# Pairing the probability-times-value matmuls of two sets, and adding zero-weight matmuls, in a planned attention kernel

## Chip, cores, metric

One core of one Trainium2 chip. The time is device microseconds of one execution; each experiment was executed several times on a chip, beside the kernel before. A program on one core gets its state (fast or slow) from its own spread; all executions quoted here are fast ones, except one of e2's four, which was slow and is left out, and the single execution of e3, whose state is unknown. The granted clock is the share of full TensorE speed in the profile's records, 1.00 or 0.50. In the profile PE is TensorE, PEld its weight loads, ACT ScalarE, DVE VectorE and POOL GpSimd.

## The reference, cut to what matters

```python
# B=1, S=2048, D=512, H=32 heads of Dh=16; inputs and weights normal * 0.05, bf16
q, k, v = split(x @ A_wqkv)
a = softmax(q k^T * Dh**-0.5) v  @ A_wo           # full attention, 32 heads x 2048 x 2048
b = attention over 8 keys at distance 0,2,..,14 @ B_wo   # local, dilated
g = sigmoid((x * gate_w).sum(-1, keepdims=True))
out = g * a + (1 - g) * b
```

Full attention is 32 x 2048 x 2048 exponentials. The work is cut in 32 periods (a chunk of 512 queries times a group of four heads). A period has 64 units, each 128 keys x 512 queries of one head.

## The kernel before

A small event-driven planner in Python (class `Plan`) runs while the program is built. Jobs are generators; they ask for an engine with a priority and a planned duration, and the order in which the planner serves them becomes the fixed program order of each engine. The timelines below show PE in that order, and semaphores in the built program keep the data right.

- Scores (QK). Sets of three and of two units alternate. The matmuls of one set stand in different 32-row strips of the array and run together: in the trace of the kernel before the three of a set start within 9 ns (median), and at half clock three take 0.61 us by the profile, a single one 0.60. Three PSUM banks hold a three-unit set ("ring" A), two hold a two-unit set (ring B); each ring exists once, so the next scores of three wait until the exponential of the last three has ended.
- Exponential on ScalarE (ACT), 1536 or 1024 columns at once, into a tile `pT`.
- PV. The matmuls of a set stand in different 32-column strips (three start within 7 ns, median), and accumulate in one bank `acc`. Below, QK3 and PV2 are the scores of a three-unit set and the PV of a two-unit set, and so on.
- Projections (the matmuls that make q, k and v from x, and the output) are put in between where the plan finds room.
- A fourth unit ("rider") may go to VectorE (DVE), which computes its exponential in four operations into a tile `pd`.

```python
class Plan:
    def advance(self, gen, t, val):       # resume a job whose own time is t
        while True:
            req = gen.send(val)
            ...
            if op == "wait":              # an event: later of the two times
                ...; t = max(t, ev.time); continue
            if op == "now":
                val = t; continue
            ...                           # an engine: stand in its list, ready at t
            self.ready[eng].append([prio, self.seq, t, gen, dur, fn, ...]); return

    def run(self):
        while True:
            ...                           # choose engine and job with the earliest start st
            self.now = st
            ...
                x[5]()                    # fn: emits the instructions
                self.free[nm] = st + x[4]
                self.advance(x[3], st + x[4] + self.LAT[nm], None)   # at once, with a time to come

    def pv_job(p, items, res, prio, act=True):
        yield ("wait", ev_acc[p])
        for t, j, _ in items:
            yield ("wait", ev_v[(i, t)])
        dur = SW + MM                     # 0.11 for a change of kind + 0.22 for a stream
        def f():
            ...                           # the set's matmuls, and finished pd units of other strips
        yield ("pe", prio, dur, f)
        yield ("rel", res[0], res[1])     # give the pT tile back

    def act_tail(k, parts, rname, rslot, ring, n):
        ...
        yield ("act", k, 0.074 + 0.4267 * n, f)           # the exponential
        yield ("rel", rname, rslot)
        for q_, (p, us) in enumerate(parts):
            yield ("spawn", pv_job(p, items, ...))
```

Of the kernel before, what the change touches and what calls it, by code (L numbers as in the profile page):

```python
# [47 lines left out]
class Plan:  # L48
# [11 lines left out]
        self.now = 0.0  # L60

    held = {"job": 0}
    cap_job = 2
    refill = 0.56
    patience = 6.0
# [18 lines left out]
    def advance(self, gen, t, val):  # L84
        while True:
# [40 lines left out]
            self.ready[eng].append([prio, self.seq, t, gen, dur, fn, req[4] if len(req) > 4 else None, t])  # L126
            return

    def gate(self, need):

        if need is None:
            return 0.0
        if not self.slots[need] or self.held["job"] >= self.cap_job:
            return None
        return min(x[0] for x in self.slots[need])
# [8 lines left out]
    def run(self):  # L144
        while True:
            best = None
            for e, lst in self.ready.items():
                rs = []
                for x in lst:
                    g_ = self.gate(x[6])  # L150
                    if g_ is not None:
                        rs.append(max(x[2], g_))
                if rs:
                    st = max(self.free[e], min(rs))
                    if best is None or st < best[0]:
                        best = (st, 1, e)
            for r, lst in self.reqs.items():
                if lst and self.slots[r]:
                    st = max(min(x[0] for x in self.slots[r]), min(x[2] for x in lst))
                    if best is None or st <= best[0]:  # L160
                        best = (st, 0, r)
            if best is None:
                return
            st, kind, nm = best
            self.now = st
            if kind == 0:
                lst = self.reqs[nm]
                x = min(y for y in lst if y[2] <= st + 1e-9)
                lst.remove(x)
                s = min(y for y in self.slots[nm] if y[0] <= st + 1e-9)  # L170
                self.slots[nm].remove(s)
                self.advance(x[3], st, s[1])
            else:
                lst = self.ready[nm]
                ok = [y for y in lst if y[2] <= st + 1e-9 and self.gate(y[6]) is not None
                      and self.gate(y[6]) <= st + 1e-9]
                x = min(ok, key=lambda y: (y[0], y[1]))
                if nm == "pe" and not self.fits(x, st):
                    for y in ok:
                        y[2] = max(y[2], st + 0.1)  # L180
                    continue
                lst.remove(x)
                if x[6] is not None:
                    slot = self.take(x[6], st)
                    self.held["job"] += 1
                    x[5](slot)
                else:
                    x[5]()
                if CFG_DEBUG:
                    LOG.append((st, x[4], nm, getattr(x[3], '__name__', '?'), x[0]))  # L190
                self.free[nm] = st + x[4]
                self.advance(x[3], st + x[4] + self.LAT[nm], None)
# [3 lines left out]
def kernel(  # L196
# [53 lines left out]
    def mm(out_, lhsT, rhs, start, stop, **kw):  # L250
        return PE.matmul(out_, lhsT=lhsT, rhs=rhs, start=start, stop=stop, **kw)
# [21 lines left out]
    z32 = const.tile([128, 32], BF16, name="z32")  # L273
    ones_t = const.tile([128, QW], BF16, name="ones_t")
# [47 lines left out]
    P = Plan(["pe", "act", "dve", "pool", "sp"])  # L322
# [10 lines left out]
    P.resource("accS", 2)  # L333
    MM = 0.22
    SW = 0.11
    VP = 0.66
    EXP_PRIO = 60

# [12 lines left out]
    NP = len(periods)  # L351
# [4 lines left out]
    ev_v = {}  # L356
# [15 lines left out]
    def k_job(i, sc, rel, prio):  # L372
# [5 lines left out]
        def pe(s):  # L378
            w.open(s, [128, QW])
            for c in range(DC):  # L380
                mm(w.t[:], wkp[:, c, i].rearrange("p j d -> p (j d)"), xT[:, c, sc * QW:(sc + 1) * QW],
                   c == 0, c == DC - 1)
        yield ("pe", prio, 4 * MM + SW, pe, "w")
        kt = kt_all[:, i, sc * QW:(sc + 1) * QW]
        yield ("dve", prio, VP, lambda: V.tensor_scalar(out=kt, in0=w.t[:], scalar1=kbias[:, 0:1], scalar2=None,
                                                        op0=ALU.add))
        yield w.close()
        yield ("dve", prio, VP, lambda: V.tensor_reduce(out=kmax_all[:, i, sc:sc + 1], in_=kt, axis=AX.X,
                                                        op=ALU.max, apply_absolute_value=True))
# [12 lines left out]
    def v_job(h0, h1, tb, TB, rel, prio):  # L402
# [18 lines left out]
        for t0 in range(0, TB, step):  # L421
            yield ("pe", prio, one * step + SW, pe(t0, t0 + step)) + (("w",) if t0 == 0 else ())
        yield ("dve", prio, VP, lambda: V.tensor_copy(out=vp_all[:, tb:tb + TB, h0:h1, 0:DH],
                                                      in_=w.t[:].rearrange("p t (h d) -> p t h d", d=DH)))
# [7 lines left out]
    def q_job(p, rel, prio):  # L432
# [8 lines left out]
        def pe(s):  # L441
            w.open(s, [128, QW])
            for c in range(DC):
                mm(w.t[:], wqp[:, c, i].rearrange("p j d -> p (j d)"), xT[:, c, c_ * QW:(c_ + 1) * QW],
                   c == 0, c == DC - 1)
        yield ("pe", prio, 4 * MM + SW, pe, "w")
        st = {}

        def absq():
            st["a"] = work.tile([128, QW], BF16, name="absq", tag="absq", bufs=1)  # L450
            hi = w.t[:].bitcast(I16).rearrange("p (n two) -> p n two", two=2)[:, :, 1]
            V.tensor_scalar(out=st["a"][:].bitcast(I16), in0=hi, scalar1=0x7FFF, scalar2=None, op0=ALU.bitwise_and)
        yield ("dve", prio, VP, absq)
        yield ("wait", ev_sel[i])
        yield ("pe", prio, MM + SW, lambda: mm(w.t[:], selk_all[:, i, :], st["a"][:], False, True,
                                               skip_group_check=True))

        def evac():
            qt = work.tile([128, QW], BF16, name="qt", tag="qt", bufs=3)
            V.tensor_scalar(out=qt[:], in0=w.t[:], scalar1=QSC, scalar2=qbias[:, 0:1], op0=ALU.mult, op1=ALU.add)  # L460
            qt_tiles[p] = qt
        yield ("dve", prio, VP, evac)
        yield w.close()
# [32 lines left out]
    act_left = [4 * NT] * NP  # L496
    row_left = [[NT] * 4 for _ in range(NP)]
    pdq = [[] for _ in range(NP)]
    nset = [0]
    ndve = [0]  # L500
    DV_MIN = 12
    flying = [0]

    def rem(p):
        return sum(len(d) for d in pend[p])

    def ready(ev, t):
        return ev.time is not None and ev.time <= t
# [5 lines left out]

    def pv_job(p, items, res, prio, act=True):

        i = periods[p][1]
        yield ("wait", ev_acc[p])
        for t, j, _ in items:
            yield ("wait", ev_v[(i, t)])  # L520
        dur = SW + MM

        def f():
            if p not in acc_tiles:
                acc_tiles[p] = ps.tile([128, QW], FP32, tag="acc", bufs=1, name="acc")
                for c4 in range(4):
                    mm(acc_tiles[p][32 * c4:32 * c4 + 32], z32[:], ones_t[:], True, False,
                       tile_position=(0, 32 * c4))
            acc = acc_tiles[p]
            now = P.now  # L530
            if act:
                act_left[p] -= len(items)
            js = [j for _, j, _ in items]
            todo = list(items)
            for e in list(pdq[p]):
                if e[0] <= now and (act_left[p] == 0 or e[2] not in js) and ready(ev_v[(i, e[1])], now):
                    pdq[p].remove(e)
                    js.append(e[2])
                    todo.append(e[1:4])
                    P.slots["pd"].append((now + dur, e[4]))  # L540
            if act_left[p] == 0:
                for e in pdq[p]:
                    P.spawn(pv_job(p, [e[1:4]], ("pd", e[4]), 0.9, False), e[0])
                pdq[p].clear()
            for t, j, pt in todo:
                pv_left[p] -= 1
                row_left[p][j] -= 1
                mm(acc[32 * j:32 * j + DH + 1, :], vp_all[:, t, 4 * i + j, :], pt, False, row_left[p][j] == 0,
                   tile_position=(0, 32 * j))
        yield ("pe", prio, dur, f)  # L550
        yield ("rel", res[0], res[1])
        if pv_left[p] == 0:
            pv_left[p] = -1
            yield ("spawn", post_job(p))
# [19 lines left out]
    def act_stream():  # L574
        while front[0] < NP:
# [28 lines left out]
            ring = ps.tile([128, 3 if k % 2 == 0 else 2, QW], FP32, tag=rname, bufs=1, name="ring")  # L604
            dur = SW + MM

# [38 lines left out]
    def dve_unit(p, t, j, s, ds, wt, n):  # L645
# [8 lines left out]
        def e23(a):  # L654
            ta = st["ta"]
            V.scalar_tensor_tensor(out=ta[:], in0=ta[:], scalar=a, in1=lo, op0=ALU.add, op1=ALU.mult)
        yield ("dve", pr, VP - 0.05, e1)
        yield ("dve", pr, VP - 0.05, lambda: e23(A2))
# [369 lines left out]
    if CFG_DEBUG:  # L1028
        import os
        import pickle  # L1030
        pickle.dump(LOG, open("/tmp/plan.pkl", "wb"))
        left = {k: [(y[0], y[3].__name__) for y in v] for k, v in P.ready.items() if v}
        left.update({k: [(y[0], y[3].__name__) for y in v] for k, v in P.reqs.items() if v})
        print("plan ends", {e: round(v, 1) for e, v in P.free.items()}, "dve units", ndve[0], "sets", nset[0], left)
        if os.environ.get("PLANONLY"):
            raise SystemExit

# [34 lines left out]
```

## Time and profile before

| | before |
|---|---|
| time, median of 2 | 999.62 us |
| mean granted clock | 0.827 |
| first exponential / tail after the last one | 36 us / 12 us |
| ACT's gaps in between, summed from starts and ends in the trace | 100.4 us |
| of these, gaps that ended while the clock was half | 45.6 us |
| pair of exponentials (3 + 2 units), median at full clock | 2.25 us (2.235 us without a projection) |

A gap is counted whole, by the clock at its end, and the stretch before the first clock record as half clock. By the share of each gap that lay in half clock it is 63.5 us.

The head of the profile page of the kernel before (a third execution, 1004.99 us): span, busy time per engine, and three rows of the picture in 40 slices (busy tenths of PE and ACT, granted clock in tenths).

```profile
span 1003.2 us, 14401 instructions
...
PE 856.1 (85%) x5408; PEld 271.8 (27%) x5408; DVE 745.7 (74%) x1282; ACT 856.1 (85%) x759; POOL 582.6 (58%) x543
...
PE   2888899988889789898888888999888888888995
...
ACT  0479489898989989988989998899898999998895
...
PEclk9998979899977878868687988667778888887686
```

PE and ACT are equally busy on paper, but a busy PE at half clock is a slow PE: scores and the PV behind them start 0.54 us apart there (490.54 and 491.08 us), 0.32 at full clock (457.94 and 458.26 us). ACT is what bounds: 371 pairs at 2.235 us are 829 us. The groups of instructions of the kernel before (busy us, mean ns | idle before, and who ended most of it):

```profile
L241 ACT ACTIVATE pT<-ring 128x1536 bf16<-128x1536 f32 x741 | 851.2, 1257 | 121.5 <-PE ring L241 54.5
L241 PE MATMUL ring<-qt,kt_all 32*128 32x512 bf16 x1853 | 339.3, 449 | 109.1 <-ACT pT L241 105.2
L241 PE MATMUL acc<-pT,vp_all 128*17 128x512 bf16 x1853 | 334.1, 446 | 1.1 <-ACT pT L241 1.1
```

The timeline of PE in the kernel before, at half clock (start us, duration us, instruction, count, and in brackets the idle time before it):

```profile
490.54 0.61 PE L241 MATMUL ring<-qt,kt_all 32*128 32x512 bf16 x3
491.08 0.60 PE L241 MATMUL acc<-pT,vp_all 128*17 128x512 bf16 x3
491.62 0.61 PE L241 MATMUL ring<-qt,kt_all 32*128 32x512 bf16 x2
492.16 0.60 PE L241 MATMUL acc<-pT,vp_all 128*17 128x512 bf16 x2
492.80 0.61 PE L241 MATMUL ring<-qt,kt_all 32*128 32x512 bf16 x3
```

Read the starts: QK3, PV3, QK2, PV2 come 0.54 us apart. The pair repeats after 2.26 us, of which 4 x 0.54 = 2.16 us are used, so at half clock a projection (four matmuls, 1.82 us from 461.06 us to the next scores) finds no room and holds ACT up (the exponential at 463.59 us came after a gap of 1.18 us).

And the clock changes in steps: in the clock records of this trace all changes lie whole multiples of 3.413 us apart. Stretches of 3.41 us of the kernel before, cut where the clock records change (PE busy, weight loads, DVE, ACT, POOL, then the granted clock):

```profile
457.16:460.57 3.41, 1.94 (x21) 0.79 (x19) 2.65 (x4) 3.41 (x4) 3.41 (x4) 1.00 0.00 0
460.57:463.99 3.41, 3.41 (x18) 0.72 (x15) 2.38 (x4) 2.23 (x3) 3.33 (x4) 0.50 0.00 0
463.99:467.40 3.41, 3.21 (x27) 1.03 (x25) 2.67 (x5) 3.32 (x4) 3.18 (x4) 1.00 0.05 20
```

Here a step in which PE was busy 1.94 of 3.41 us is followed by one at half clock, in which a projection comes and ACT is busy only 2.23 us; that step, with PE busy throughout, is followed by full clock again.

### The profile page before, as it was taken

The numbers are of one execution on the slowest core, as the hardware profiler recorded it, in microseconds if no ns is written. First come the engines' busy times: TensorE is split into PE (matmuls) and PEld (weight loads), VectorE is DVE, ScalarE is ACT, GpSimd is POOL, SyncE is SP. The second block draws the span as 40 slices with busy tenths as digits, with TensorE's granted clock in tenths as the row PEclk, the third lists the DMA queues.
The fourth block names the chain that finished last, engine by engine and source line by source line (L and its number), as shares of the span: only waits on it lengthen the run. The fifth ranks groups of instructions, "written<-read, shape, count | busy, mean of one in ns | idle before, by whom it ended". The sixth has DMA issues, their size and how long they took to land.

```text
span 1003.2 us, 14401 instructions
## 1 busy us (share of the span) xinstructions
PE 856.1 (85%) x5408; PEld 271.8 (27%) x5408; DVE 745.7 (74%) x1282; ACT 856.1 (85%) x759; POOL 582.6 (58%) x543
## 2 busy tenths in 40 slices
PE   2888899988889789898888888999888888888995
PEld 1332433222222222222222222222222222222221
DVE  3566877586778777778877877887777776788775
ACT  0479489898989989988989998899898999998895
POOL 4004694300976928689739598829394949493600
PEclk9998979899977878868687988667778888887686
DMA  9004010001220020313100330202003020310000
GB/s 252 1 2 147 1 43 2 1 12 42 95 80 26 12 90 11 95 48 90 49 11 1 100 95 6 96 1 65 31 1 95 6 74 32 100 43 1 1 1 22
DMA packets 50006, 47.09 MB, mean 47 GB/s; under 512 B 9984, under 2 KB 47360, under 8 KB 49936
## 3 DMA queue, kind: packets, MB, share of 16 engines
q1 hardware_dynamic: 46240, 41.98, 13.8%
q10 hardware_dynamic: 3696, 4.20, 1.5%
q8 instruction: 42, 0.69, 0.3%
q14 instruction: 28, 0.23, 0.1%
HBM read 37.75 MB, written 6.32 MB: 44 GB/s over the span
## 4 chain that ended last, share of the span: by engine, by line
PE 41%; ACT 34%; issue 16%; DVE 6%; DMA 2%; SPq 0%; ACTq 0%; DVEq 0%
ACT pT L241 34%; PE ring L241 13%; PE acc L241 12%; DMA xT<-in_A_x_dram 2%; DVE ta L241 2%; DVE accS L241 1%; DVE kt_all L241 1%; ACT lg L241 0%; DVE vp_all L241 0%; DVE qt L241 0%; DVE lg L241 0%; DVE pd L241 0%; DVE kmax_all L241 0%; PE w_3662 L241 0%; PE w_9217 L241 0%
## 5 line engine op out<-in xcount | busy, mean ns | idle before, releaser
L241 ACT ACTIVATE pT<-ring 128x1536 bf16<-128x1536 f32 x741 | 851.2, 1257 | 121.5 <-PE ring L241 54.5
L241 PE MATMUL ring<-qt,kt_all 32*128 32x512 bf16 x1853 | 339.3, 449 | 109.1 <-ACT pT L241 105.2
L241 PE MATMUL acc<-pT,vp_all 128*17 128x512 bf16 x1853 | 334.1, 446 | 1.1 <-ACT pT L241 1.1
L241 POOL TENSOR_TENSOR prod<-vsh,lg 128x512 f32<-128x512 bf16 x128 | 136.6, 1099 | 195.6 <-issue 133.0
L241 POOL TENSOR_TENSOR prod<-prod 128x512 f32<-128x512 f32 (+1 forms) x208 | 240.0, 1167 | 6.3
L241 POOL TENSOR_TENSOR prod<-ksh,qb 128x512 f32<-128x512 bf16 x128 | 143.7, 1155 | 155.2 <-DVE qb L241 143.6
L241 PEld LDWEIGHTS <-kt_all 32*128 32x128 bf16 x2048 | 104.4, 93 | 349.0 <-issue 343.4
L241 PEld LDWEIGHTS <-vp_all 128*17 128x17 bf16 x2048 | 70.4, 89 | 205.1 <-issue 203.6
L241 PE MATMUL acc<-pd,vp_all 128*17 128x512 bf16 x195 | 86.7, 471 | 0.0
L241 PEld LDWEIGHTS <-xT 128*128 128x128 bf16 x512 | 36.0, 109 | 45.0 <-issue 36.4
L241 DVE COPY accS<-acc 128x512 f32<-128x512 f32 x32 | 22.0, 687 | 8.2 <-PE acc L241 7.6
L241 DVE TENSOR_REDUCE kmax_all<-kt_all 128x1 f32<-128x512 bf16 x32 | 21.7, 679 | 0.4
L241 PEld LDWEIGHTS <-wkp 128*128 128x128 bf16 x128 | 11.1, 104 | 37.1 <-issue 18.0
L241 POOL TENSOR_TENSOR obb<-ob,prod 128x512 bf16<-128x512 f32 x16 | 20.3, 1272 | 1.2
L241 POOL TENSOR_TENSOR ob<-prod 128x512 f32<-128x512 f32 x16 | 20.3, 1269 | 1.3
L241 PEld LDWEIGHTS <-wqp 128*128 128x128 bf16 x128 | 12.3, 115 | 26.1 <-issue 20.3
L241 PE MATMUL acc<-ones_t,z_85 128*32 128x512 bf16 x128 | 15.2, 464 | 1.0 <-DVE accS L241 0.5
L241 POOL TENSOR_TENSOR lg<-prod 128x128 f32<-128x128 f32 x32 | 13.7, 429 | 2.5
L241 ACT ACT_TABLE_LOAD x1 | 1.3, 1283 | 12.2 <-DMA xT<-in_A_x_dram 12.2
L241 PE MATMUL w_136<-xT,wkp 128*128 128x512 bf16 x4 | 1.9, 619 | 11.3 <-DMA xT<-in_A_x_dram 11.3
L241 DVE TENSOR_TENSOR lg<-lg,mx 128x256 f32<-128x256 f32 x16 | 9.0, 561 | 0.1
L241 DVE RECIPROCAL rden<-rden 128x16 f32<-128x16 f32 x32 | 8.0, 249 | 0.6
(1390 smaller groups left out, 1143.7 us busy)
## 6 DMA issues: line engine op xcount, KB each, us to landing
ksh<-kv_scr SPq DMA_DIRECT2D x16, 1024.0 KB, 5.8
vsh<-kv_scr SPq DMA_DIRECT2D x16, 1024.0 KB, 7.3
kv_scr<-kvs SPq DMA_DIRECT2D x16, 256.0 KB, 2.0
out_dram<-osb SPq DMA_DIRECT2D x16, 128.0 KB, 1.7
bw<-in_B_wqkv_dram ACTq DMA_DIRECT2D x1, 1536.0 KB, 14.5
wraw<-in_A_wqkv_dram ACTq DMA_DIRECT2D x2, 512.0 KB, 6.2
wv<-in_A_wqkv_dram ACTq DMA_DIRECT2D x1, 512.0 KB, 10.1
bwo<-in_B_wo_dram ACTq DMA_DIRECT2D x1, 512.0 KB, 8.1
```

The lines of the kernel that those rows point to most:

```text
L241: return chain_on(self._key, f(*a, **k))
```

## The change

Its intent: PV groups of three and two units become one group of five (two rounds in the column strips), so that PE changes less often between row-tiled and column-tiled matmuls; and where a group starts and PE has streamed little in the last 3 us of the plan, one matmul with zero weights is added, to keep the clock up.

```diff
+    streamed = deque()
+    def quiet(self, window):
+        while self.streamed and self.streamed[0][0] < self.now - window:
+            self.streamed.popleft()
+        return sum(d - 0.11 for _, d in self.streamed)
 ...
+    WARM = 0.47
+    held_pv = [[] for _ in range(NP)]
 ...
     def pv_job(p, items, res, prio, act=True):
         ...
+        if act:
+            act_left[p] -= len(items)
+            if len(items) == 3 and act_left[p] > 0:
+                held_pv[p].append((items, res))
+                return
         dur = SW + MM
+        fin = [res]
         def f():
 ...
+                for its, r in held_pv[p]:
+                    todo = list(its) + todo
+                    fin.append(r)
+                held_pv[p].clear()
 ...            (the group's matmuls, in rounds; finished pd units where a round has room)
+            extra = MM * (max(cnt) - 1)
+            if P.quiet(3.0) + MM * max(cnt) < WARM * 3.0 and max(row_left[p]) > 0:
+                j = max(range(4), key=lambda j_: row_left[p][j_])
+                mm(acc[32 * j:32 * j + 32, :], z32[:], ones_t[:], False, False, tile_position=(0, 32 * j))
+                extra += MM
+            return extra
         yield ("pe", prio, dur, f)
-        yield ("rel", res[0], res[1])
+        for r in fin:
+            yield ("rel", r[0], r[1])
```

In the program order, which can be read before any run, the runs of one matmul kind on PE fall from 1687 to 1214, zero matmuls rise from 128 (they open each accumulator) to 137, sets fall from 741 to 737 and VectorE units rise from 195 to 206.

More of the change, by code (lines that the diff above doesn't have):

```diff
@@ L185, in run @@
                     self.held["job"] += 1
-                    x[5](slot)
+                    more = x[5](slot)
                 else:
-                    x[5]()
+                    more = x[5]()
+                if isinstance(more, float):
+                    x[4] += more
+                if nm == "pe":
+                    self.streamed.append((st, x[4]))
                 if CFG_DEBUG:
@@ L502 @@
     flying = [0]
+    njunk = [0]
+    held_pv = [[] for _ in range(NP)]
     def rem(p):
@@ L530, in f @@
             now = P.now
+            todo = list(items)
             if act:
-                act_left[p] -= len(items)
-            js = [j for _, j, _ in items]
-            todo = list(items)
+                for its, r in held_pv[p]:
+                    todo = list(its) + todo
+                    fin.append(r)
+                held_pv[p].clear()
+            cnt = [sum(1 for x in todo if x[1] == j) for j in range(4)]
+            most = max(cnt)
             for e in list(pdq[p]):
-                if e[0] <= now and (act_left[p] == 0 or e[2] not in js) and ready(ev_v[(i, e[1])], now):
+                if e[0] <= now and (act_left[p] == 0 or cnt[e[2]] < most) and ready(ev_v[(i, e[1])], now):
                     pdq[p].remove(e)
-                    js.append(e[2])
+                    cnt[e[2]] += 1
                     todo.append(e[1:4])
-                    P.slots["pd"].append((now + dur, e[4]))
+                    fin.append(("pd", e[4]))
             if act_left[p] == 0:
@@ L544, in f @@
                 pdq[p].clear()
-            for t, j, pt in todo:
+            seen = [0] * 4
+            order = []
+            for x in todo:
+                order.append((seen[x[1]], x))
+                seen[x[1]] += 1
+            for _, (t, j, pt) in sorted(order, key=lambda y: y[0]):
                 pv_left[p] -= 1
@@ L549, in f @@
                    tile_position=(0, 32 * j))
+            extra = MM * (max(cnt) - 1)
[3 more added lines that the diff above has]
+                extra += MM
+                njunk[0] += 1
+            return extra
         yield ("pe", prio, dur, f)
-        yield ("rel", res[0], res[1])
+        for r in fin:
+            yield ("rel", r[0], r[1])
         if pv_left[p] == 0:
@@ L1033 @@
         left.update({k: [(y[0], y[3].__name__) for y in v] for k, v in P.reqs.items() if v})
-        print("plan ends", {e: round(v, 1) for e, v in P.free.items()}, "dve units", ndve[0], "sets", nset[0], left)
+        print("plan ends", {e: round(v, 1) for e, v in P.free.items()}, "junk", njunk[0], "dve units", ndve[0], "sets", nset[0], left)
         if os.environ.get("PLANONLY"):
```

## The prediction

> **What bounds the kernel now.** ScalarE's exponentials. In the engine table PE and ACT are each busy 856 of 1003 us; by start times in the trace a pair of exponentials (three units, then two) repeats every 2.235 us while the clock is full (1.331 + 0.904 us, medians), so 371 pairs need about 829 us. The stretches by window show no exponential before 36 us, and 12 us of tail. ACT's gaps between sum to 100 us: 26 before 150 us (12.4 of it in one stall at 101 us), 35 later at full clock, 40 later at half clock. PE is late: the waits view names PE's ring first.
>
> Mean granted clock 0.827, changing in steps of 3.41 us. Counting columns streamed per step (concurrent matmuls merged) against the full-rate maximum: half-clock steps up to 0.39 stay cold, those above about 0.41 are followed by full clock; full-clock steps below about 0.40 by half clock. [...] Four streams of 0.213 us per 2.26 us are 0.38, so a stretch without projection work falls cold, and the next projection (four matmuls, 1.82 us cold) then holds ACT up by 1.2 to 1.7 us.
>
> **What the change does.** (a) In program order QK3, PV3, QK2, PV2 becomes QK3, QK2, PV5. Streams stay the same (PV5 takes two rounds), but the runs of one matmul kind on PE fall from 1687 to 1214. In the timeline, streams of different kinds start 0.32 us apart warm and 0.54 cold, against 0.215 and 0.43 for the same kind, so a change costs about 0.11 us [...]. Estimate: 473 x 0.11 = 52 us less PE time. Only late stretches count: a backlogged cold pair falls from 2.16 to 1.94 us.
> (b) Zero matmuls: ones_t matmuls go from 128 to 137, so nine were added. As a PV group starts, the planned last 3 us already hold enough.
> (c) Sets fall from 741 to 737, DVE units rise from 195 to 206: about 5 us less ACT work.
> (d) Against: QK2 and two PV rounds now stand together. Cold, about 1.5 us from QK2's start to the next QK3, while ACT releases that ring after about 1.35 us: an estimated 0.08 us lost per cold pair that has no projection, some 6 us.
> (e) Streaming is lumpier (one stream, then three), so some cold steps should rewarm and some warm ones fall. Clock roughly 0.83 to 0.88.
>
> **Sum.** Of about 100 us ACT gaps roughly 30 should go, 5 us less ACT work, 6 us given back: about 970 us, 3% faster. Range 952 to 988. Chances: faster by over 2%: 0.72; within 2%: 0.26; slower: 0.02.
>
> **Signs.** ACT gaps total 65 to 80 us, losing most at half clock; first exponential still at 36 us; "PE ring" waits shrink; nine more zero matmuls; QK-to-QK starts 0.43 cold; clock not raised by more than 0.06; cold no-projection pairs at about 2.3 us instead of 2.26.
>
> **What would make it wrong.** If cold steps grow more frequent (clock under 0.80), projections meet half clock more often and the gain vanishes. If rewarming is much easier, the gain is larger (below 952). If held PV groups delay the accumulator's hand-over, or P tiles run out, ACT waits on PV.

"Cold" is half clock, "warm" full clock. The limits of 0.39 to 0.41 are my count in the trace of the kernel before, put too sharply: the steps overlap, half-clock ones rose from 0.36 on and stayed up to 0.44 (figures in the last section).

## More of the kernel before

The experiments ran on four different chips; the kernel before had medians of 1000.9 to 1002.9 us beside them.

Score matmuls wait for ACT (the ring must come free); PV matmuls wait for practically nothing, 1.1 us in the whole run: when PE comes to them, their probabilities are already there.

## The result

| | before | after |
|---|---|---|
| time, median of 2 | 999.62 us | 1151.2 us |
| mean granted clock | 0.827 | 0.765 |
| ACT's gaps | 100.4 us | 225.6 us |
| of these, ended at half clock | 45.6 us | 134.4 us |
| pair, median at full / half clock | 2.25 / 2.26 us | 2.54 / 3.18 us |

The ratio is 1.152 (95% interval 1.147 to 1.157). Ratios here are the mean time of one kernel's fast runs over that of the other's of the same rounds, so they are not quite the ratio of the medians. Executions over 1.5% slower than the fastest of the same kernel are left out of the means.

The same head of the page, changed kernel:

```profile
span 1148.8 us, 14309 instructions
...
PE 832.3 (72%) x5351; PEld 238.6 (21%) x5417; DVE 766.2 (67%) x1326; ACT 876.9 (76%) x755; POOL 582.5 (51%) x543
...
PE   3878776787788677677767776767678776667775
...
ACT  0577877887778878877778877778788877877794
...
PEclk8589988988768957766578967658688966766695
```

PE and ACT are now both idle a quarter of the time. Two engines that idle that much may be waiting for each other in turn, and the groups and the chain below show that here they are. The same three groups:

```profile
L252 ACT ACTIVATE pT<-ring 128x1536 bf16<-128x1536 f32 x737 | 872.0, 1236 | 247.8 <-PE ring L252 149.0
L252 PE MATMUL acc<-pT,vp_all 128*17 128x512 bf16 x1842 | 294.3, 471 | 252.5 <-ACT pT L252 251.9
L252 PE MATMUL ring<-qt,kt_all 32*128 32x512 bf16 x1842 | 329.2, 469 | 23.0 <-ACT pT L252 21.8
```

The wait has moved. Before, scores waited for ACT (105 us) and PV for nothing; now PV waits 252 us for an exponential and scores hardly wait, because they stand behind PV in PE's order. PE of the changed kernel in the timeline, at half clock:

```profile
506.45 0.60 PE L252 MATMUL acc<-pT,vp_all 128*17 128x512 bf16 x4 [1.18 <-ACT pT L252]
...
507.41 1.03 PE L252 MATMUL ring<-qt,kt_all 32*128 32x512 bf16 x5
509.57 1.03 PE L252 MATMUL acc<-pT,vp_all 128*17 128x512 bf16 x5 [1.13 <-ACT pT L252]
510.53 1.03 PE L252 MATMUL ring<-qt,kt_all 32*128 32x512 bf16 x5
```

And ACT of the changed kernel in the timeline, in the same stretch:

```profile
504.95 2.37 ACT L252 ACTIVATE pT<-ring 128x1536 bf16<-128x1536 f32 x2 [1.24 <-PE w_4972 L252]
508.07 2.37 ACT L252 ACTIVATE pT<-ring 128x1536 bf16<-128x1536 f32 x2 [0.76 <-PE ring L252]
```

The two exponentials of a pair merge into one line, the three-unit one first. The scores of both sets are done at 508.4 (507.41 + 1.03); then PE stands still until 509.57, just after the end of the *three-unit* exponential that began at 508.07 and took 1.46 us, and only then runs the PV group, and the next scores after it. The chain of waits of the changed kernel shows the cycle:

```profile
508.07 1.46 ACT pT L252
509.57 1.03 PE acc L252 x5
510.60 0.57 PE ring L252 x3
511.20 0.04 issue
511.25 1.46 ACT pT L252
```

508.07 to 511.25 is 3.18 us: three-unit exponential, PV group, scores, one after the other; only the two-unit exponential runs beside the PV group. A group of set k and set k+1 need not wait there: set k+2's exponential is the one that it waits for.

### The profile page after: what moved, and what is told of

It reads as the page before. It is cut to its first block, busy times and chain, and to the rows that moved or that the text cites. A ratio compares the mean times of both kernels' runs of the same rounds, so it can differ in the third digit from the quotient of the medians.

```text
span 1148.8 us, 14309 instructions
## 1 busy us (share of the span) xinstructions
PE 832.3 (72%) x5351; PEld 238.6 (21%) x5417; DVE 766.2 (67%) x1326; ACT 876.9 (76%) x755; POOL 582.5 (51%) x543
## 4 chain that ended last, share of the span: by engine, by line
PE 49%; ACT 41%; issue 5%; DVE 2%; DMA 2%; ACTq 0%; SPq 0%; DVEq 0%
ACT pT L252 41%; PE acc L252 22%; PE ring L252 14%; DMA xT<-in_A_x_dram 2%; DVE ta L252 1%; DVE accS L252 0%; ACTq L252 0%; ACT lg L252 0%; DVE kt_all L252 0%; PE w_4473 L252 0%; PE w_7101 L252 0%; DVE vp_all L252 0%; PE w_8057 L252 0%; PE w_7751 L252 0%; PE w_5777 L252 0%
## 5 line engine op out<-in xcount | busy, mean ns | idle before, releaser
L252 ACT ACTIVATE pT<-ring 128x1536 bf16<-128x1536 f32 x737 | 872.0, 1236 | 247.8 <-PE ring L252 149.0
L252 PE MATMUL acc<-pT,vp_all 128*17 128x512 bf16 x1842 | 294.3, 471 | 252.5 <-ACT pT L252 251.9
L252 PE MATMUL ring<-qt,kt_all 32*128 32x512 bf16 x1842 | 329.2, 469 | 23.0 <-ACT pT L252 21.8
L252 PEld LDWEIGHTS <-kt_all 32*128 32x128 bf16 x2048 | 69.8, 95 | 318.6 <-issue 315.3
L252 PE MATMUL acc<-pd,vp_all 128*17 128x512 bf16 x206 | 94.9, 500 | 0.0
L252 PEld LDWEIGHTS <-xT 128*128 128x128 bf16 x512 | 33.7, 106 | 40.6 <-issue 30.9
L252 PE MATMUL acc<-ones_t,z_85 128*32 128x512 bf16 x137 | 19.7, 449 | 2.0 <-DVE accS L252 1.5
L252 PEld LDWEIGHTS <-wqp 128*128 128x128 bf16 x128 | 12.9, 122 | 28.2 <-issue 26.3
L252 DVE TENSOR_REDUCE ssum<-lg 128x32 f32<-128x256 f32 x16 | 6.7, 416 | 4.8 <-ACT lg L252 4.7
```

The lines of the kernel that those rows point to most:

```text
L252: return chain_on(self._key, f(*a, **k))
```

## Why it waits: two theories

*Theory W, wrong partner.* A finished engine request resumes its job at once, but with a time to come: `advance(x[3], st + x[4] + ...)`. In the kernel before this is harmless, since the job's next act is to stand in an engine's list with that time. The change puts an act with no time in between: `held_pv[p].append(...)`. So the moment an exponential is *placed* in the plan, its three-unit set lies in the list, over a microsecond before it is done in the plan, and the next PV group to be emitted takes it. (The kernel before already guards the DVE units against this: it asks `now = yield ("now",)`, stores that time with the unit in `pdq`, and a PV group compares it.) The plan's own log, with an added line for each QK and PV group, shows it (planned times of the builder, not the chip's):

```
438.62  exponential of set 342 (3 units), planned to 439.98
438.70  QK of set 343 (2 units)
439.03  PV of set 341 (2 units) together with five units: the held three are set 342's
```

The plan believes that this group runs at 439.03. But its matmuls read set 342's probabilities, so in the built program it waits for that exponential, and what stands behind it on PE waits as well: in the timeline above a PV group waits 1.13 us, and the scores behind it start at 510.53, 0.96 us after the group's own start. The waits in the program order agree. Kernel before, then changed kernel (first matmul of each group only):

```
before:  Matmult ring<-qt,kt_all  [waits Activation]      after:  Matmult ring<-qt,kt_all  [waits PE]
         Matmult acc<-pT,vp_all                                   Matmult ring<-qt,kt_all  [waits Activation]
         Matmult ring<-qt,kt_all  [waits Activation]              Matmult acc<-pT,vp_all   [waits Activation]
         Matmult acc<-pT,vp_all                                   Matmult ring<-qt,kt_all  [waits PE]
```

Before, 706 of 715 PV groups have no wait for ACT of their own: the PV of set k stands right behind the scores of set k+2, and these scores have waited for the same exponential, that of set k, which frees their ring. After, 332 of 400 PV groups wait for ACT themselves, and the three-unit scores behind them mostly need no such wait (56 of 368 have one): by then the exponential that frees their ring has been waited for.

*Rival B, burst and clock.* The merging itself is at fault: one score stream and two PV rounds in a row are too long at half clock (my point (d)), and the lumpy streaming lowers the clock (my point (e)). *Rival Z:* the zero matmuls do harm.

## Experiments

### e1: the same order without the wait

Where a group takes a three-unit set whose exponential is not done by the plan's time, its matmuls read a constant tile. Every instruction on PE stands in the same place (compared line by line); 936 matmuls, 312 groups, are changed, and only 23 of the 400 PV groups still wait for ACT in the program, against 332.

```diff
-                held_pv[p].append((items, res))
+                now = yield ("now",)
+                held_pv[p].append((now, items, res))
 ...
-                for its, r in held_pv[p]:
-                    todo = list(its) + todo
+                for t_, its, r in held_pv[p]:
+                    todo = [(t, j, pt if t_ <= now else ones_t[:]) for t, j, pt in its] + todo
```

> The changed kernel, with PE's instruction order the same in every place, but where a PV group takes a three-unit set whose exponential, by the plan's own time, is not done yet (312 groups), those three matmuls read a constant tile in place of the probabilities: they wait for nothing, and the result is wrong on purpose. Theory W (the group took the set of the next exponential, so PE stands still until it ends, and the scores for the exponential after it stand behind the group): about 950 to 1000 us, 'acc waits for pT' falls from 252 us to under 30. Rival B (a burst of one score stream and two PV rounds is too long at half clock, and the lumpy streaming keeps the clock low): still over 1100 us, since order and streams are the same.

Measured: 945.2 us (944.9 to 945.5), ratio to before 0.941 (0.938 to 0.945), clock 0.839. Groups of e1:

```profile
L252 ACT ACTIVATE pT<-ring 128x1536 bf16<-128x1536 f32 x737 | 847.4, 1283 | 67.8 <-PE w L252 30.4
...
L252 PE MATMUL acc<-pT,vp_all 128*17 128x512 bf16 x906 | 254.2, 442 | 0.9 <-ACT pT L252 0.6
```

The same order and the same streams are over 200 us faster, even a little faster than I expected. The wait is the cause of the loss; rival B, which the same order would still show, is out. One caution: the comparison with the reference called this kernel correct although its arithmetic is wrong. From the reference, q and k have a spread of about 0.05 x 0.05 x sqrt(512) = 0.057, so a scaled score is about 0.057 x 0.057 x 4 x 0.25 = 0.003 and every exponential is close to 1: ones in place of probabilities stay within its tolerance. Correctness here says little about which data a PV matmul read.

### e2: each set with its own partner

```diff
-                held_pv[p].append((items, res))
+                now = yield ("now",)
+                held_pv[p].append((now, items, res))
 ...
-                for its, r in held_pv[p]:
-                    todo = list(its) + todo
-                    fin.append(r)
-                held_pv[p].clear()
+                for e in list(held_pv[p]):
+                    if e[0] <= now:
+                        held_pv[p].remove(e)
+                        todo = list(e[1]) + todo
+                        fin.append(e[2])
```

> The changed kernel, mended: a held set carries the time at which its exponential ends, and a PV group takes only sets whose time has come, so set k goes with set k+1 as the change says. Theory W: about 955 to 990 us, like the constant tile, correct. Rival B: over 1100 us. Pair period at full clock 2.24 us instead of 2.54, at half clock about 2.3 instead of 3.18.

Measured, three fast executions: 944.8 us (937.7 to 947.3); a fourth, 952.1 us, was slow. Ratio 0.939 (0.934 to 0.945), clock 0.847, ACT's gaps 39.3 us. Groups of e2:

```profile
L252 ACT ACTIVATE pT<-ring 128x1536 bf16<-128x1536 f32 x737 | 846.1, 1294 | 61.7 <-PE w L252 30.9
L252 PE MATMUL ring<-qt,kt_all 32*128 32x512 bf16 x1842 | 328.2, 436 | 119.0 <-ACT pT L252 110.1
...
L252 PE MATMUL acc<-pT,vp_all 128*17 128x512 bf16 x1842 | 266.8, 441 | 0.3 <-ACT pT L252 0.2
```

PE of e2 in the timeline, at full clock:

```profile
745.72 0.39 PE L252 MATMUL ring<-qt,kt_all 32*128 32x512 bf16 x2
746.04 0.60 PE L252 MATMUL acc<-pT,vp_all 128*17 128x512 bf16 x5
746.68 0.39 PE L252 MATMUL ring<-qt,kt_all 32*128 32x512 bf16 x3
747.60 0.39 PE L252 MATMUL ring<-qt,kt_all 32*128 32x512 bf16 x2 [0.52 <-ACT pT L252]
747.61 0.38 PE L252 MATMUL w<-qt,kt_all 32*128 32x512 bf16 x1
```

The order of kinds is still QK3, QK2, PV5, but the group of sets k and k+1 now mostly (284 of 395 groups in the program order) stands behind the scores of k+2 and k+3. PV waits 0.2 us, scores wait for ACT as they should, and what the change meant to do makes the kernel 6% faster than before. e1 and e2 differ by less than e2's spread, so the wrong partner explains the whole loss. The pair takes 2.235 us at full clock (median); at half clock without a projection 2.35 us (2.37 with them), a little more than before's 2.26 us. That is what the burst of rival B would cost, and it is small; no run tests the burst alone.

Where the gain comes from can be counted in the traces. Pairs that touched half clock and held a projection or a transpose took together 108 us more than 2.235 us each in the kernel before (75 pairs) and 35 us more in e2 (36 pairs). All of the gain is there, where the prediction had looked for most of it.

### e3: the changed kernel without its nine zero matmuls

```diff
-            if P.quiet(3.0) + MM * max(cnt) < WARM * 3.0 and max(row_left[p]) > 0:
+            if False and max(row_left[p]) > 0:
```

> The changed kernel without its nine zero matmuls, sets held as in it. Theories W and B: 1145 to 1157 us, same as with them. Rival Z (the zero matmuls do harm or good): a change of over 10 us.

Without the zero matmuls the plan's times shift, so the later order is not line by line that of the changed kernel, but the wrong pairing is the same. Measured: 1142.7 us, a single execution (state unknown), clock 0.767. It is 2 us below my range and 0.7% below the changed kernel's 1151.2; with one execution I read no effect into it. Rival Z is out as the cause of the loss.

### e4: zero matmuls alone

```diff
-            if len(items) == 3 and act_left[p] > 0:
+            if False:
```

With smaller groups the test fires 106 times. With the test off as well, the PE order built is line by line that of the kernel before, so e4 differs from it by the zero matmuls and what they move in the plan.

> The other part of the change alone: no set is held, the zero matmul stays with its test (it now fires 106 times, as the groups are smaller). Theories W and B: 985 to 1005 us, the time before within 2%, granted clock 0.83 to 0.86. Rival Z (zero matmuls cost): over 1020 us.

Measured: 987.1 us (982.7 to 989.1), ratio 0.982 (0.979 to 0.986), clock 0.866. The second half of the change, alone, is worth almost 2% (clear of zero; whether it is over 2% is not). In the whole change it could not show it: the test fired only nine times.

### e5: more zero matmuls in the changed kernel, inside the groups

```diff
-    WARM = 0.47
+    WARM = 1.2
```

> The changed kernel, wrong pairing kept, with the zero matmul's threshold raised from 0.47 to 1.2 (377 zero matmuls in groups in place of 9), to part the wait's own cost from the half clock that follows it. Theory W: the wait stays (acc waits for pT still 150 us or more), but the clock rises over 0.9, so the pair repeats every 2.5 to 2.8 us, not 3.18, and the time falls to about 1020 to 1070 us; it does not reach the kernel before. If the time stays at 1140 or over, the clock had no share in the loss.

Measured: 1143.2 us (1132.7 to 1145.0), ratio 1.139 (1.132 to 1.145), clock 0.793, half-clock pairs still 3.18 us. My expectation missed: the clock hardly rose. The 377 zero matmuls stand in the group, on the chain itself, about one per pair. Five streams of 0.213 us (half of the 0.427 us between streams of one kind at half clock) in 3.18 us are 0.335 of full rate, below the 0.40 or so above which most half-clock steps of the kernel before were followed by full clock (a line there sorts 95 of 102 steps). By the letter this would say that the clock had no share; it says only that this experiment did not hold the clock up. e9 and e10 were made for that.

### e6, e7, e8: how many zero matmuls does the mended kernel want

e6 is e2 with the test off (as in e3); e7 and e8 are e2 with `WARM = 0.6` and `0.8` (125 and 253 zero matmuls in groups).

> The mended kernel with no zero matmul in groups: the hold alone. If the seven zero matmuls of the mended one are worth nothing: 938 to 955 us, within 1% of it. The gain over the kernel before is then the fewer changes of matmul kind and the units moved to VectorE.

> The mended kernel with the threshold at 0.6 (125 zero matmuls in groups in place of 7): the granted clock rises from 0.85 to 0.88 or more, and the ACT gaps left at half clock (17 us of 39) shrink: 925 to 945 us.

> The same with the threshold at 0.8 (253 zero matmuls): clock over 0.92; PE has some room at full clock (a pair needs about 1.1 of 2.235 us): 922 to 945 us. If zero matmuls stand in the way of scores, slower than with 0.6.

| | zeros in groups | time (range) | ratio to before | clock |
|---|---|---|---|---|
| e2 (three fast) | 7 | 944.8 (937.7 to 947.3) | 0.939 | 0.847 |
| e6 | 0 | 942.0 (940.2 to 947.7) | 0.942 | 0.860 |
| e7 | 125 | 946.7 (945.7 to 948.3) | 0.945 | 0.883 |
| e8 | 253 | 947.5 (943.6 to 952.4) | 0.946 | 0.889 |

The hold alone (e6) has the whole gain. Zero matmuls in the groups raise the clock, less than I expected of e8, and the time does not follow: e7 and e8 land just above their ranges. Why is not settled; e8's gaps that ended at half clock are only 14.0 us against 22.5 in e6, but its gaps in all are 45.5 against 41.5, so what the clock gave was lost elsewhere in ACT's gaps.

### e9, e10: the wait without the half clock

Two (e9) or three (e10) zero matmuls stand behind the scores of 302 of the 369 two-unit sets of the changed kernel, where PE idles 1.13 to 1.19 us anyway (timeline of the changed kernel). The plan is not told, so all else keeps its order (compared line by line).

```diff
                     ndve[0] += 1
+                q = units[0][0]
+                if len(units) == 2 and units[-1][0] == q and q in acc_tiles and max(row_left[q]) > 0:
+                    j = max(range(4), key=lambda j_: row_left[q][j_])
+                    for _ in range(NZ):
+                        mm(acc_tiles[q][32 * j:32 * j + 32, :], z32[:], ones_t[:], False, False,
+                           tile_position=(0, 32 * j))
```

> The changed kernel, wrong pairing and order kept, with two zero matmuls put behind the scores of nearly every two-unit set, where PE stands idle for 1.2 us until the exponential ends, so that they stay off the chain; the plan is not told of them. It parts the wait from the half clock better than a higher threshold did, whose zeros stood in the group, on the chain. Streams per pair go from four to six, which is 0.40 of full rate in a 3.18 us pair: steps should warm. Theory W: clock 0.90 or more, pairs nearly all at about 2.54 us, time 1050 to 1100 us, still slower than before by the wait alone.

> The same with three zero matmuls: 0.47 of full rate in a 3.18 us pair, 0.59 in a 2.54 us pair. Clock over 0.95, pairs at 2.54 us, 1040 to 1090 us. If the time stays over 1130 us in spite of such a clock, the half clock had no share in the loss.

Measured: e9 1048.0 us (1046.5 to 1049.8), ratio 1.045 (1.041 to 1.048), clock 0.978; e10 1063.4 us (1061.9 to 1064.7), ratio 1.059, clock 0.985. Both as expected (e9 2 us below its range). The row of the granted clock and the PV matmuls' group, from the page of e9:

```profile
PEclk9999999999999999999899999999999999999998
...
L252 PE MATMUL acc<-pT,vp_all 128*17 128x512 bf16 x1842 | 240.6, 389 | 141.0 <-ACT pT L252 140.5
```

PE of e9 in the timeline:

```profile
506.32 0.61 PE L252 MATMUL acc<-pT,vp_all 128*17 128x512 bf16 x5 [0.74 <-ACT pT L252]
506.86 0.76 PE L252 MATMUL ring<-qt,kt_all 32*128 32x512 bf16 x5
507.56 0.61 PE L252 MATMUL acc<-ones_t,z 128*32 128x512 bf16 x2
508.86 0.61 PE L252 MATMUL acc<-pT,vp_all 128*17 128x512 bf16 x5 [0.70 <-ACT pT L252]
```

The wait is still there, but the pair now repeats after 2.54 us (506.32 to 508.86). Adding work to the stalled engine took about 103 us off the time. So the loss has two parts of about equal size: the serial cycle itself at full clock (e9 stays about 106 us over e6), and the half clock, which came with the idle PE (clock 0.765, against 0.978 with the zero matmuls in the idle time) and which stretched each turn of the cycle from 2.54 to 3.18 us. Against e11 below, the mended kernel held at full clock as well, the serial cycle costs 116 us, and the half clock then some 103 us in the changed kernel and 10 us in the mended one. The split is rough, since the runs were on different chips and the zero matmuls also stand before projections; e10, with more of them and a higher clock, is 15 us slower than e9.

### e11: the mended kernel, held at full clock

e6 with one zero matmul behind the scores of 303 of the 368 *three*-unit sets (the edit of e9 with `len(units) == 3` and `NZ = 1`).

> The mended kernel without the threshold test, with one zero matmul behind the scores of nearly every three-unit set, where PE has room until the exponential before ends: five streams per 2.235 us pair are 0.48 of full rate, so it should stay warm. Clock over 0.95; half-clock gaps nearly gone. If the half clock still costs the mended kernel what its gaps there show (about 18 us), 920 to 935 us; if the zeros delay projections as much as they help, 938 to 950 us.

Measured: 932.4 us (931.6 to 934.2), ratio 0.932 (0.928 to 0.936), clock 0.954. From the page of e11:

```profile
span 931.4 us, 14962 instructions
...
PEclk9599999999989998799999999999989999999998
...
L252 ACT ACTIVATE pT<-ring 128x1536 bf16<-128x1536 f32 x737 | 845.9, 1296 | 58.4 <-PE w L252 30.0
```

It is the best of all kernels here, 6.8% faster than before, and its executions lie closer together than e2's. Its 303 zero matmuls stand in the slack behind the scores of three (a gap of 0.52 us in e2's timeline above); e8's 253 in the PV groups left the time where it was. The place tells here, though number and place were not varied apart.

## Why the prediction was wrong, point by point

- *What bounds the kernel before, the clock's steps, half-clock projections*: right. The clock mattered in both directions: with the clock held up off the chain, e11 (clock 0.954) is some 10 us faster than e6 and e9 (0.978) wins back half the loss.
- *(a) "In program order QK3, PV3, QK2, PV2 becomes QK3, QK2, PV5"*: this is the step that failed. The order of kinds was right, but the step left out PV5's wait: I took PV5 for the group of its own pair, as the change's description says, and read the order without the waits. The five units were a two-unit set and the *next* three-unit set. Two readings that were possible before any run would have told: the waits in the program order (most PV groups had gained one), and the code, where an act without a time was put between a resumed job and its next request. The trace then showed PV's wait for ACT at 252 us against 1.1, and with it a serial cycle: a pair took 2.54 us at full clock and 3.18 us at half clock in place of 2.25 and 2.26. The 52 us that fewer changes of kind were to save on PE could not count while PE stood waiting.
- *The size of (a)*: with the partners right, e2 removes 61 of 100 us of ACT's gaps, where I had put 30, and lands at 945 us, below my range of 952 to 988. The term of about 30 us was mis-sized by half. The loss went from the pairs in which half clock met a projection: such pairs fell from 75 to 36, and one wholly at half clock from 3.97 to 3.42 us. How much of that is the clock, which rose to 0.847 without being asked, I did not part.
- *(b) Nine zero matmuls, almost nothing*: right, as far as e3's single execution shows.
- *(c) Less ACT work*: about right; in e2, where nothing stalls, ACT is busy 849.7 us against 856.1 before. DVE, with more units, was busy 761.0 of 935.9 us (81%).
- *(d) A longer burst at half clock*: seen only in e2, and agrees in size: 2.35 us per half-clock pair without a projection, 2.3 predicted; that the burst is the reason is not shown.
- *(e) Clock 0.83 to 0.88*: wrong for the changed kernel (0.765), whose PE was busy only 72% of the time, against 85% before; with zero matmuls in its idle time it had 0.978 (e9). e2 had 0.847. Of the listed dangers, "clock under 0.80" came true, but as the follower of the wait, not as the first cause; it then cost about half of the loss. "Held PV groups delay the accumulator's hand-over, or P tiles run out" did not come true: ACT's waits for PV fell from 12.9 to 8.0 us in the waits view.
- *Signs*: first exponential at 36 us and nine zero matmuls held; the gaps (225.6 us, 65 to 80 predicted) and "PE ring waits shrink" failed: ACT's wait for the ring rose from 54.5 to 149.0 us. That line names the scores, which were late because they stood behind a waiting PV group: in e1, with that wait gone and the order kept, it is 27.7 us.

## What to carry to other kernels

When a change reorders an engine's program, read the waits with the order. Here the PV groups gained waits (1.1 us became 251.9), the scores behind them came late, and the profile named the innocent scores (ACT's wait for the ring rose from 54.5 to 149.0 us). In a planner whose jobs are resumed early with a time to come, any state that a job writes without a time (a list, a counter) leaks the future into the plan, so give it a time and compare it. And in this kernel an idle TensorE was punished twice, by the wait (some 106 us) and by the half clock (some 103 us, e9); zero matmuls helped where they stood in slack (e9: 1151.2 to 1048.0 us, e11: 932.4 against e6's 942.0) and hardly on the chain (e5: 1143.2 us).

## What the traces show of the clock and of changes of kind

- Here the clock fell although PE's gaps were short. In the step 457.16 to 460.57 us of the kernel before, the longest gap in PE's timeline is 0.63 us and half clock follows; in the changed kernel's steady stretch gaps of 1.13 to 1.19 us came with half clock throughout.
- Activity counted in columns streamed per step of 3.41 us, concurrent tiles once, against full rate (512 columns in 0.213 us, half of the 0.427 us at half clock): in the kernel before, half-clock steps that stayed had a median of 0.38 and those that rose 0.43; full-clock steps that fell had a median of 0.38, those that stayed 0.62. The groups overlap (steps rose from 0.36 on and stayed at half clock up to 0.44). A line at 0.40 sorts 95 of 102 half-clock and 166 of 177 full-clock steps there, but only 54 of 84 half-clock steps in e2 and 50 of 77 in e4, so it is a rough limit of this one trace. Four 512-column streams per 2.26 us (0.38) lie just below that line.
- A change of matmul kind: starts are 0.32 us apart with a change and 0.215 without at full clock, 0.54 and 0.43 at half clock: about 0.11 us at either clock.
- Added zero matmuls shortened two kernels: 106 of them took 1.8% off the kernel before (e4), about 600 took 9% off the stalled one (e9).
